# Attention's output turned by float32 products with stacked unit matrices, in place of transposes and additions

## The chip, the cores and the metric

One core of one Trainium2 chip runs the whole program. The metric is the device time of one execution in microseconds; lower is better. The kernel before was timed three times, and one more execution was profiled.

## The reference, cut to what matters

Four batches of eight heads of attention with rotary positions (sequence 576, head size 64) feed two gated layers over 2304 tokens. What the change touches is the last line of attention and the turn to tokens by features:

```python
scores = scale * np.matmul(q_rot, k_rot.transpose(0, 1, 3, 2))
scores = scores - np.max(scores, axis=-1, keepdims=True)
attn = np.exp(scores)
attn = attn / (np.sum(attn, axis=-1, keepdims=True) + 1e-09)
return np.matmul(attn, v).astype(np.float32)
...
x = np.ascontiguousarray(attn_out.transpose(0, 2, 1, 3)).reshape(B * S, H * D)
x = _moe_ref(x=x, **moe_kwargs)
return _moe2_ref(x=x, **moe2_kwargs)
```

## The kernel before, in words

**Precision.** TensorE multiplies float32r values, a shortened float32. To keep float32's precision, each operand is split into two float32r halves, hi (a rounding, on ACT) and lo (the rest, a subtraction on DVE), and a product is made of three products of halves (`PASS`: hi by hi, hi by lo, lo by hi). Transposes move whole float32 values (L598, L679, L709, L749, L771, L1226), except those at L1608, which are of float32r.

**Attention's stage.** The 32 heads are worked as 16 pairs `p`. A pair has nine tiles `t` of 128 rows of scores: four of each head, and tile 4, the left-over 64 rows of both. For each tile: S (scores, into one of two double banks of PSUM), M (negative row maximum, DVE), E (exponential and row sum, ACT), T (four transposes of P, into one of four PSUM banks `ps_g`), H and Lo (the split of P into `pt`, ACT and DVE). LP, LH and LL do the same for the 64 left-over columns. The Q and K of the next pair are turned (q0 to q2: qp on TensorE, qh on ACT, ql on DVE) and moved to their places by DMAs (q1d, q2d, L617).

**O.** For head `h` and half `hf` of the 576 queries, PV (L735) has as its stationary operand V's hi columns beside V's lo columns (64 + 64), and as its moving operand P. So its result has V's feature on the partitions: 64 rows of P by V's hi, and below them 64 rows of P by V's lo, which must be added to give O. OS (L740, ACT) copies it to `osb`, 128 x 576. O (L746 to L749) turns it: four transposes of 128x128 into one bank, after which each row is a query and has 64 hi features and 64 lo features. OA (L751, ACT) copies the lo features, 256 a partition, to `x`; OR (L754, DVE) adds the hi features to them and is the last to read the bank. OL (L768) turns the left-over 64 queries of both heads (two transposes), and OLR (L774, DVE) adds their halves in one reduction. RS (POOL) and RR (DVE) make 1/sum of each row, X (L790, POOL) multiplies, XD (L798) sends the pair's 128 features to `xD` in DRAM by two DMAs on SP's queue.

**Order.** The order is written by hand: `ORDER` (L18) gives each step a time in tiles, and step `n` of pair `p` is issued at `9 * p + ORDER[n]`, sorted by this time; each engine then works its own instructions in this order. In a pair's frame O0 stands at 14.022, OL at 15.595 and O1 at 16.188, so within the next pair at 5.0, 6.6 and 7.2; the S0 of the pair after that stands at 6.93 (9 - 2.067), right behind OL. The last pair's steps past the end of attention go to a planner (`Plan`), with the costs in `TAIL` (L74) and the dependences listed there; it keeps TensorE's order and arranges the other engines' work between the first products of the next layer. `tail_op` (L1061) also tells the planner which PSUM bank a step holds.

**After attention** TensorE multiplies for the two layers, in products of 384 or 256 columns (L1099, L1125, L1345, L1492, L1652, L1725); ACT, DVE and POOL split and combine.

Of the kernel before, what the change touches and what calls it, by code (L numbers as in the profile page):

```python
# [8 lines left out]
F32 = mybir.dt.float32  # L9
# [4 lines left out]
ALU = mybir.AluOpType  # L14
AX = mybir.AxisListType
# [15 lines left out]

ONCE = {"WF.0": 1.47, "WF.1": 1.48, "W0.0": 10.0, "W1.0": 12.2, "W2.0": 13.4, "W0.1": 11.6, "W3.0": 16.7,
# [41 lines left out]
TAIL = {"H": ("ACT", 0.6, ()), "Lo6": ("DVE", 0.65, ("H6",)), "Lo7": ("DVE", 0.65, ("H7",)), "Lo8": ("DVE", 0.65, ("H8",)),  # L74
# [5 lines left out]
PRI = 100  # L80
FIRST = {"q2p": -0.115, "q0p": -0.114, "q2h": -0.112, "q0h": -0.111, "q2l": -0.06, "q0l": -0.05, "q2d": -0.03,
    "q1p": 1.2, "q1h": 1.25, "q1l": 1.44, "q1d": 1.45}
# [5 lines left out]
def f(ap):  # L88
    return ap.bitcast(F32)
# [187 lines left out]
def kernel(  # L277
# [21 lines left out]
    nc = tc.nc  # L299
    B, H, S, D = q.shape  # L300
# [25 lines left out]
    const = ctx.enter_context(tc.tile_pool(name="const", bufs=1))  # L326
# [16 lines left out]
    idn = f(idr)  # L343
    g_sb = const.tile([128, DM], F32, name="g")
    cst = const.tile([128, 4], F32, name="cst")
    half, three, one, eps = [cst[:, i:i + 1] for i in range(4)]

    def opener(st):
# [28 lines left out]
    tab_p = pool("tab", 1)  # L377
    rightx = ctx.enter_context(ExitStack())
    rpool = lambda name, bufs: rightx.enter_context(tc.tile_pool(name=name, bufs=bufs, side="right", reuse_waits="tile"))
    ss_p = rpool("ss", 2)  # L380
    mem = []

    def grow():
# [130 lines left out]
    part = {}  # L514
# [122 lines left out]
    s_ps, s_max, p_sb, sums, t_ps, l_ps, pv_ps, osb, xt, o_ps, rs_t = [{} for _ in range(11)]  # L637
# [88 lines left out]
    def head_steps(h):  # L726
        def pv(hf):
            sl = slice(hf * HS, (hf + 1) * HS)

            def PV(p):  # L730
                vs = vss[p]
                ps = pv_ps[p, h, hf] = ps_g.tile([128, 512], F32, tag="g", name="pv")
                mm = [(vs[:, h, c], pt[:, 1 - h, i, c, sl]) for c in range(4) for i in range(2)] + [(vs[:, h, 4], lt[:, 1 - h, sl])]
                for i, (l, r) in enumerate(mm):
                    nc.tensor.matmul(ps[:, 0:HS], lhsT=l.rearrange("p s d -> p (s d)"), rhs=r, start=(i == 0), stop=(i == 8))  # L735

            def OS(p):
                if (p, h) not in osb:
                    osb[p, h] = osb_p.tile([128, S], F32, tag="o", name="osb")
                nc.scalar.copy(out=osb[p, h][:, sl], in_=pv_ps.pop((p, h, hf))[:, 0:HS])  # L740

            part[f"PV{h}{hf}"], part[f"OS{h}{hf}"] = PV, OS

        pv(0), pv(1)

        def O_(p):  # L746
            ps = o_ps[p, h] = ps_g.tile([128, 4, 128], F32, tag="g", name="op")
            for r in range(4):
                nc.tensor.transpose(ps[:, r], osb[p, h][:, r * 128:(r + 1) * 128], idn)  # L749

        def OA(p):  # L751
            nc.scalar.copy(out=xh_(p)[:, 0:4, h], in_=o_ps[p, h][:, :, D:128])

        def OR(p):  # L754
            nc.vector.tensor_tensor(out=xh_(p)[:, 0:4, h], in0=o_ps.pop((p, h))[:, :, 0:D], in1=xh_(p)[:, 0:4, h], op=ALU.add)

        part[f"O{h}"], part[f"OA{h}"], part[f"OR{h}"] = O_, OA, OR

    def xh_(p):
        if p not in xt:  # L760
            xt[p] = x_p.tile([128, 5, 2 * D], F32, tag="x", name="x")
        return xt[p].rearrange("p r (h d) -> p r h d", d=D)

    head_steps(0), head_steps(1)


    @step
    def OL(p):  # L768
        ps = o_ps[p, 2] = ps_g.tile([128, 4, 128], F32, tag="g", name="op")
        for h in range(2):  # L770
            nc.tensor.transpose(ps[:, h], osb[p, h][:, S - 128:S], idn)  # L771

    @step
    def OLR(p):  # L774
        nc.vector.tensor_reduce(out=xh_(p)[:, 4], in_=o_ps.pop((p, 2))[:, 0:2].rearrange("q r (s d) -> q r d s", s=2), axis=AX.X, op=ALU.add)  # L775

    @step
    def RS(p):
# [83 lines left out]
    ident = p_p.tile([128, S], F32, tag="p", name="ident")[:, 0:128]  # L862
    make_identity(nc, ident)
    nc.vector.tensor_copy(out=idr, in_=ident)
    man = ExitStack()
    man.enter_context(tc.manual_schedule())
    load(0)
# [86 lines left out]
    for p in range(NP):  # L954
        for n_, t in ORDER.items():
            d = 2 if n_ in ("ra", "rb", "rc", "rd", "lq", "lv") else 1 if n_[0] in "qv" else 0
# [37 lines left out]
    for u in range(6, 9):  # L994
        i, s = divmod(u, 3)
# [18 lines left out]
    def key(sp, i, n=1):  # L1014
        return sp, i, i + n
# [39 lines left out]
    def gslot():  # L1055
        gb[0] += 1
        return key("g", (gb[0] - 1) % 4)
# [3 lines left out]
    def tail_op(n_):  # L1061
        eng, dur, deps = TAIL["H" if n_[0] == "H" else n_]
        wr = []
        if n_ in ("PV11", "PV10", "O0", "OL", "O1"):
            tails["slot", n_] = gslot()
            wr = [tails["slot", n_]]
        for a, b in (("OS11", "PV11"), ("OS10", "PV10"), ("OA0", "O0"), ("OR0", "O0"), ("OLR", "OL"), ("OA1", "O1"), ("OR1", "O1")):
            if n_ == a:
                wr = [tails["slot", b]]
        if n_ == "XD":  # L1070
            wr = [key("xD", 13, 5)]
        tails[n_] = plan(eng, dur, lambda: part[n_](NP - 1), (), wr, dep=[tails[d] for d in deps if d in tails], kb=288 if n_ == "XD" else 0)
# [4 lines left out]
    def tail_to(n_):  # L1077
        while names and (n_ is None or n_ in names):
            tail_op(names.pop(0))
# [10 lines left out]
    def products_b(si, i, n, s):  # L1090
        sl = gslot()
        w, x = wgv[n], xg[i]

        def go():
            p_ = ps_ap[si, s] = ps_g.tile([128, 512], F32, tag="g", name="mm")[:, 0:CH]
            j = 0
            for c in range(KC):
                for a, b_ in PASS:
                    nc.tensor.matmul(p_, lhsT=w.ap[:, a, s, c * 128:(c + 1) * 128], rhs=x.ap[:, b_, c, :], start=(j == 0), stop=(j == 3 * KC - 1))  # L1099
                    j += 1  # L1100
        mark(plan("PE", 12 * MM, go, [w.part(s, 4), w.part(2 + s, 4), x.part()], [sl]))
        return sl
# [309 lines left out]
    for si, (i, n) in enumerate(steps):  # L1412
        if si == 0:
            units_to(9)
        g = products_b(si, i, n, 0)
# [404 lines left out]
```

## Time and profile before

| | us |
|---|---|
| median of three runs | 1051.91 |
| lowest, highest | 1051.77, 1054.71 |
| the profiled execution | 1052.25 |
| its span, first to last instruction | 1050.5 |
| attention's stage in it (pairs in full flow) | 27 to 312 |

The profile shows one execution. "Busy" is the time in which an engine works on at least one instruction; PE is TensorE's products, PEld its weight loads, which run beside them. A product's end is modelled, so neighbours overlap in the rows, and the distance between starts says more than the length. "<-" after a wait names what ended it. `op` is the PSUM tile of O and OL, `x` the result of OA, OR and OLR.

### The profile page before, as it was taken

The page shows a single profiled execution, that of the slowest core. Times are in us where ns is not written, and L with a number is a line of the kernel's source. Part 1 is how long each engine was busy: PE and PEld are TensorE (multiplying, and loading weights), DVE is VectorE, ACT ScalarE, POOL GpSimd, SP SyncE. Part 2 cuts the span into 40 slices and gives each one's busy share as a digit, 9 for nine tenths or more (in the row PEclk, how much of TensorE's full clock was granted, in tenths as well). Part 3 has the DMA queues.
Part 4 walks back from the last instruction along what each step waited for, and adds up shares of the span by engine and source line. Part 5 has one row for each costly group of instructions (what it writes and reads, how often), then busy time and mean ns, then how long its engine had stood idle before and what let it go on. Part 6 is the DMA issues. An engine that isn't in the chain of part 4 may idle for free.

```text
span 1050.5 us, 19662 instructions
## 1 busy us (share of the span) xinstructions
PE 1032.5 (98%) x6969; PEld 1022.7 (97%) x6969; DVE 810.4 (77%) x1394; ACT 656.6 (63%) x1442; POOL 378.1 (36%) x495
## 2 busy tenths in 40 slices
PE   7999999999999999999999999999999999999998
PEld 6999999999999999999999999999999999999997
DVE  7999999999987966779888778432576567998653
ACT  6898999898978654457666666332554344575430
POOL 7878888889610002543212230001522111410000
PEclk9999999999999999999999999999999999999999
DMA  6777877777669887279897967571342326445761
GB/s 159 210 203 195 221 174 183 185 190 181 176 212 308 280 261 235 81 237 314 292 355 246 317 206 226 185 238 46 106 158 106 154 73 214 176 148 211 270 219 61
DMA packets 125986, 210.41 MB, mean 200 GB/s; under 512 B 19136, under 2 KB 71744, under 8 KB 125888
## 3 DMA queue, kind: packets, MB, share of 16 engines
q1 hardware_dynamic: 125456, 208.71, 63.8%
q8 instruction: 55, 0.90, 0.4%
q10 hardware_dynamic: 432, 0.44, 0.1%
q14 instruction: 43, 0.35, 0.1%
HBM read 117.62 MB, written 63.96 MB: 173 GB/s over the span
## 4 chain that ended last, share of the span: by engine, by line
PE 87%; DVE 6%; DMA 3%; ACT 2%; issue 1%; SPq 1%; DVEq 0%; ACTq 0%
PE ps L1345 33%; PE mm L1099 10%; PE ps L1492 10%; PE ps L1725 9%; PE s L662 5%; PE acc L1125 5%; PE pv L735 4%; PE ps L1652 4%; PE tp L679 4%; DMA ks<-xy 2%; DVE nm L667 2%; DVE pt L687 2%; PE qtp L598 1%; PE lp L709 1%; PE op L749 1%
## 5 line engine op out<-in xcount | busy, mean ns | idle before, releaser
L1032 DVE TENSOR_TENSOR v<-v 128x256 fp32r<-128x256 f32 (+8 forms) x424 | 286.4, 704 | 94.7 <-ACT v L1026 92.2
L1345 PE MATMUL ps<-v 128*128 128x384 f32 x2016 | 350.7, 334 | 0.8 <-ACT ps L1026 0.8
L1345 PEld LDWEIGHTS ps<-v 128*128 128x128 f32 x2016 | 349.3, 188 | 1.5 <-ACT ps L1026 1.5
L1032 POOL TENSOR_TENSOR v<-v 128x256 f32<-128x256 f32 (+1 forms) x140 | 136.5, 992 | 475.5 <-DVE v L1032 185.0
L1026 ACT CAST v<-v 128x256 fp32r<-128x256 f32 (+5 forms) x364 | 203.3, 589 | 129.4 <-DMA v<-uG 41.0
L1032 DVE TENSOR_TENSOR v<-ps,v 128x384 f32<-128x384 f32 (+3 forms) x162 | 89.1, 572 | 75.7 <-PE ps L1345 36.8
L1026 ACT COPY v<-ps 128x384 f32<-128x384 f32 (+2 forms) x130 | 62.4, 482 | 112.6 <-PE ps L1345 58.5
L662 PE MATMUL s<-ks,qs 128*128 128x288 f32 x640 | 119.9, 313 | 6.4 <-ACT p L673 3.0
L667 DVE TENSOR_REDUCE nm<-s 128x1 f32<-128x576 f32 x144 | 107.8, 749 | 7.7 <-PE s L662 5.4
L673 ACT ACTIVATE p<-s,nm 128x576 f32<-128x576 f32 x144 | 107.4, 746 | 9.4 <-DVE nm L667 8.6
L1099 PE MATMUL mm<-v 128*128 128x384 f32 x576 | 104.2, 335 | 0.0
L1492 PE MATMUL ps<-v 128*128 128x384 f32 x576 | 100.0, 334 | 0.0
L1099 PEld LDWEIGHTS mm<-v 128*128 128x128 f32 x576 | 99.9, 188 | 0.0
L1492 PEld LDWEIGHTS ps<-v 128*128 128x128 f32 x576 | 99.9, 188 | 0.0
L662 PEld LDWEIGHTS s<-ks,qs 128*128 128x128 f32 x640 | 89.5, 189 | 10.1 <-ACT p L673 6.1
L687 DVE TENSOR_TENSOR pt<-tp,pt 128x512 fp32r<-128x512 f32 x144 | 94.6, 681 | 0.7
L1725 PE MATMUL ps<-v 128*128 128x256 f32 x756 | 90.9, 283 | 0.0
L1725 PEld LDWEIGHTS ps<-v 128*128 128x128 f32 x756 | 90.8, 192 | 0.0
L679 PE MATMUL tp<-idr,p 128*128 128x128 f32 x576 | 81.9, 273 | 1.1 <-DVE x L775 0.7
L683 ACT CAST pt<-tp 128x512 fp32r<-128x512 f32 x144 | 82.3, 585 | 1.0 <-PE tp L679 0.2
L735 PE MATMUL pv<-pt,vs 128*128 128x288 f32 x512 | 80.9, 300 | 0.1
L735 PEld LDWEIGHTS pv<-pt,vs 128*128 128x128 f32 x512 | 70.9, 188 | 0.3 <-DVE pt L687 0.3
(131 smaller groups left out, 1263.3 us busy)
## 6 DMA issues: line engine op xcount, KB each, us to landing
ks<-xy SPq DMA_DIRECT2D x60, 288.0 KB, 5.2
v<-in_moe_w_dram SPq DMA_DIRECT2D x32, 512.0 KB, 6.3
v<-in_moe_w_out_dram SPq DMA_DIRECT2D x20, 512.0 KB, 6.0
qs<-xy SPq DMA_DIRECT2D x60, 160.0 KB, 3.3
uG<-v SPq DMA_DIRECT2D x24, 384.0 KB, 4.7
v<-uG SPq DMA_DIRECT2D x24, 384.0 KB, 3.7
uD<-v SPq DMA_DIRECT2D x12, 768.0 KB, 3.5
v<-uD SPq DMA_DIRECT2D x12, 768.0 KB, 6.6
```

The costliest lines, as they stand in the source:

```text
L662: nc.tensor.matmul(ps[:, hf, 0:HS], lhsT=l, rhs=r_[:, hf * HS:(hf + 1) * HS], start=(i == 0), stop=(i == n - 1))
L667: nc.vector.tensor_reduce(out=nm, in_=s_ps[p, t][:, :, 0:HS], axis=AX.XY, op=ALU.max, negate=True)
L673: nc.scalar.activation(out=pp.rearrange("p (a b) -> p a b", a=2), in_=s_ps.pop((p, t))[:, :, 0:HS], func=AF.Exp, bias=s_max.pop((p, t)), s ...
L679: nc.tensor.transpose(ps[:, c, :], p_sb[p, t][:, LF + c * 128:LF + (c + 1) * 128], idn)
L687: lastins["dve"] = nc.vector.tensor_tensor(out=lo, in0=src, in1=f(hi), op=ALU.subtract)
L735: nc.tensor.matmul(ps[:, 0:HS], lhsT=l.rearrange("p s d -> p (s d)"), rhs=r, start=(i == 0), stop=(i == 8))
L1026: return plan("ACT", act_us(n), lambda: nc.scalar.copy(out=o(), in_=i()), rd, wr)
L1032: lambda: eng.tensor_tensor(out=o(), in0=x(), in1=y(), op=op), rd, wr)
L1099: nc.tensor.matmul(p_, lhsT=w.ap[:, a, s, c * 128:(c + 1) * 128], rhs=x.ap[:, b_, c, :], start=(j == 0), stop=(j == 3 * KC - 1))
L1345: nc.tensor.matmul(p_(), lhsT=w[i].ap[:, a, c * 128:(c + 1) * 128], rhs=x[i].ap[:, r, c], start=(first and ch != 1 and n == 0), stop=(n == 5),
L1492: nc.tensor.matmul(ac[o][ch][0](), lhsT=w.ap[:, a, o * 128:(o + 1) * 128], rhs=u.ap[:, b_, ch], start=(j == 0 and s == 0), stop=(j == NF - ...
L1725: nc.tensor.matmul(p_()[:, k * 256:(k + 1) * 256], lhsT=u.ap[:, a, UOP[i], o * 128:(o + 1) * 128], rhs=w(b_), start=(g == 0 and s == 0 and ...
```

## The change

A constant `both` (128 x 64, float32) holds two unit matrices above each other. O and OL are no longer transposes but products: stationary operand the same 128x128 piece of `osb`, moving operand `both`. Row q, column d of the result is `osb[d, q] + osb[64 + d, q]`: turned and added at once, 64 columns a piece in place of 128. OA copies the finished 256 values; OR is gone; OLR is a copy. `both` is made by one addition of two halves of the unit matrix at the start. The pool `ss` has one buffer in place of two. The planner's list loses OR0 and OR1, and its other costs are kept.

```diff
-    "PV10": 13.085, "OS10": 13.618, "O0": 14.022, "OA0": 15.251, "OL": 15.595, "OR0": 15.671, "O1": 16.188,
-    "RR": 16.466, "lv": 16.571, "OLR": 16.975, "OA1": 16.977, "OR1": 17.165, "X": 17.215, "XD": 17.967}
+    "PV10": 13.085, "OS10": 13.618, "O0": 14.022, "OA0": 15.251, "OL": 15.595, "O1": 16.188,
+    "RR": 16.466, "lv": 16.571, "OLR": 16.975, "OA1": 16.977, "X": 17.215, "XD": 17.967}
...
-    "OR0": ("DVE", 0.4, ("OA0",)), "OL": ("PE", 0.22, ("OS01", "OS11")), "OLR": ("DVE", 0.35, ("OL",)), "O1": ("PE", 0.44, ("OS10", "OS11")),
-    "OA1": ("ACT", 0.4, ("O1",)), "OR1": ("DVE", 0.4, ("OA1",)), "RS": ("POOL", 0.6, ()), "RR": ("DVE", 0.2, ("RS",)),
-    "X": ("POOL", 1.5, ("OR0", "OR1", "OLR", "RR")), "XD": ("SP", 0.8, ("X",))}
+    "OL": ("PE", 0.22, ("OS01", "OS11")), "OLR": ("DVE", 0.35, ("OL",)), "O1": ("PE", 0.44, ("OS10", "OS11")),
+    "OA1": ("ACT", 0.4, ("O1",)), "RS": ("POOL", 0.6, ()), "RR": ("DVE", 0.2, ("RS",)),
+    "X": ("POOL", 1.5, ("OA0", "OA1", "OLR", "RR")), "XD": ("SP", 0.8, ("X",))}
...
+    both = const.tile([128, D], F32, name="both")
...
-    ss_p = rpool("ss", 2)
+    ss_p = rpool("ss", 1)
...
         def O_(p):
-            ps = o_ps[p, h] = ps_g.tile([128, 4, 128], F32, tag="g", name="op")
+            ps = o_ps[p, h] = ps_g.tile([128, 512], F32, tag="g", name="op")[:, 0:4 * D].rearrange("q (r d) -> q r d", d=D)
             for r in range(4):
-                nc.tensor.transpose(ps[:, r], osb[p, h][:, r * 128:(r + 1) * 128], idn)
+                nc.tensor.matmul(ps[:, r], lhsT=osb[p, h][:, r * 128:(r + 1) * 128], rhs=both, start=True, stop=True)
 
         def OA(p):
-            nc.scalar.copy(out=xh_(p)[:, 0:4, h], in_=o_ps[p, h][:, :, D:128])
-
-        def OR(p):
-            nc.vector.tensor_tensor(out=xh_(p)[:, 0:4, h], in0=o_ps.pop((p, h))[:, :, 0:D], in1=xh_(p)[:, 0:4, h], op=ALU.add)
+            nc.scalar.copy(out=xh_(p)[:, 0:4, h], in_=o_ps.pop((p, h)))
...
     def OL(p):
-        ps = o_ps[p, 2] = ps_g.tile([128, 4, 128], F32, tag="g", name="op")
+        ps = o_ps[p, 2] = ps_g.tile([128, 512], F32, tag="g", name="op")[:, 0:2 * D].rearrange("q (h d) -> q h d", d=D)
         for h in range(2):
-            nc.tensor.transpose(ps[:, h], osb[p, h][:, S - 128:S], idn)
+            nc.tensor.matmul(ps[:, h], lhsT=osb[p, h][:, S - 128:S], rhs=both, start=True, stop=True)
...
     def OLR(p):
-        nc.vector.tensor_reduce(out=xh_(p)[:, 4], in_=o_ps.pop((p, 2))[:, 0:2].rearrange("q r (s d) -> q r d s", s=2), axis=AX.X, op=ALU.add)
+        nc.vector.tensor_copy(out=xh_(p)[:, 4], in_=o_ps.pop((p, 2)))
...
+    nc.vector.tensor_tensor(out=both, in0=ident[:, 0:D], in1=ident[:, D:2 * D], op=ALU.add)
```

## Rows read from the trace of the kernel before

**Rows 1.** The page's first part: engines over the whole span.
```profile
PE 1032.5 (98%) x6969; PEld 1022.7 (97%) x6969; DVE 810.4 (77%) x1394; ACT 656.6 (63%) x1442; POOL 378.1 (36%) x495
```

**Rows 2.** Stretches: us, busy us of each engine (instructions), granted clock, DMA share, GB/s.
```profile
core 0: us, PE busy (x) PEld busy (x) DVE busy (x) ACT busy (x) POOL busy (x), PEclk, DMA share, GB/s
27.00:312.00 285.00, 279.81 (x2221) 273.45 (x2222) 270.80 (x479) 259.12 (x636) 219.30 (x324) 1.00 0.74 194
...
312.00:345.00 33.00, 33.00 (x199) 32.90 (x198) 27.00 (x60) 23.39 (x54) 2.06 (x2) 1.00 0.88 298
345.00:400.00 55.00, 55.00 (x336) 54.90 (x334) 42.99 (x81) 33.06 (x62) 0.00 (x0) 1.00 0.87 278
400.00:700.00 300.00, 299.24 (x1725) 298.63 (x1725) 220.93 (x392) 170.54 (x370) 75.41 (x80) 1.00 0.74 243
```

**Rows 3.** TensorE's waits, 27 to 312 us: us in total, times, longest.
```profile
PE s L662 <- DMA ks<-xy: 2.3, 4, 1.3
PE op L749 <- DVE pt L687: 0.9, 2, 0.5
PE tp L679 <- DVE x L775: 0.7, 2, 0.4
PE s L662 <- DMA qs<-xy: 0.7, 1, 0.7
PE op L771 <- DVE lt L717: 0.2, 1, 0.2
PE s L662 <- ACT p L673: 0.2, 1, 0.2
PE s L662 <- issue: 0.2, 1, 0.2
```

**Rows 4.** Instructions on tile `op`: ns least/median/most, first and last start, forms.
```profile
L749 PEld LDWEIGHTS op<-idr,osb x128: 137/139/146, 42.1 to 309.5; 128*128 128x128 f32 x128
L749 PE MATMUL op<-idr,osb x128: 270/272/332, 42.2 to 309.6; 128*128 128x128 f32 x128
L771 PEld LDWEIGHTS op<-idr,osb x32: 137/140/143, 43.8 to 309.1; 128*128 128x128 f32 x32
```

**Rows 5.** The chain that ended last, 112 to 120 us: start, us, what.
```profile
114.46 0.44 PE op L749 x4
114.89 1.19 PE pv L735 x9
116.08 0.22 PE op L771 x2
116.30 0.16 issue
116.46 0.76 PE s L662 x4
```

**Rows 6.** The chain at 879 us, and the weight loads of line 1608.
```profile
879.50 1.31 PE ps L1608 x16
...
L1608 PEld LDWEIGHTS ps<-idr,v x64: 137/140/143, 879.2 to 931.2; 128*128 128x128 f32 x64
```

**Rows 7.** The chain of the whole span: products of 384 and of 256 columns.
```profile
461.93 172.13 PE ps L1345 x990
...
954.58 90.73 PE ps L1725 x756
```

**Rows 8.** Instructions on tile `x`: ns least/median/most, first and last start, forms.
```profile
L752 ACT COPY x<-op x32: 360/372/373, 44.3 to 309.9; 128x256 f32<-128x256 f32 x32
L755 DVE TENSOR_TENSOR x<-op,x x32: 406/414/425, 45.1 to 312.4; 128x256 f32<-128x256 f32 x32
...
L775 DVE TENSOR_REDUCE x<-op x16: 362/412/415, 46.7 to 311.4; 128x128 f32<-128x256 f32 x16
```

**Rows 9.** DVE's groups by shape, 27 to 312 us: busy us, mean ns, idle before.
```profile
L607 DVE TENSOR_TENSOR xy<-qtp,xy 128x128 fp32r<-128x128 f32 x14 | 4.1, 291 | 0.5 <-ACT xy L602 0.5
```

**Rows 10.** All engines' waits, 27 to 312 us: us in total, times, longest.
```profile
ACT x L752 <- PE op L749: 6.6, 14, 1.7
```

**Rows 11.** DVE's instructions in order of time, 0 to 16 us: start, us, what, idle before.
```profile
1.45 0.16 DVE L864 CAST idr<-ident 128x128 fp32r<-128x128 f32 x1
4.16 0.69 DVE L544 TENSOR_TENSOR rot<-raw,cos 128x512 f32<-128x512 f32 x1 [2.54 <-DMA raw<-in_k_dram]
```

More of the change, by code (lines that the diff above doesn't have):

```diff
@@ L746, in O_ @@
         def O_(p):
-            ps = o_ps[p, h] = ps_g.tile([128, 4, 128], F32, tag="g", name="op")
+            ps = o_ps[p, h] = ps_g.tile([128, 512], F32, tag="g", name="op")[:, 0:4 * D].rearrange("q (r d) -> q r d", d=D)
             for r in range(4):
-                nc.tensor.transpose(ps[:, r], osb[p, h][:, r * 128:(r + 1) * 128], idn)
+                nc.tensor.matmul(ps[:, r], lhsT=osb[p, h][:, r * 128:(r + 1) * 128], rhs=both, start=True, stop=True)
         def OA(p):
-            nc.scalar.copy(out=xh_(p)[:, 0:4, h], in_=o_ps[p, h][:, :, D:128])
-        def OR(p):
-            nc.vector.tensor_tensor(out=xh_(p)[:, 0:4, h], in0=o_ps.pop((p, h))[:, :, 0:D], in1=xh_(p)[:, 0:4, h], op=ALU.add)
-        part[f"O{h}"], part[f"OA{h}"], part[f"OR{h}"] = O_, OA, OR
+            nc.scalar.copy(out=xh_(p)[:, 0:4, h], in_=o_ps.pop((p, h)))
+        part[f"O{h}"], part[f"OA{h}"] = O_, OA
     def xh_(p):
@@ L1066, in tail_op @@
             wr = [tails["slot", n_]]
-        for a, b in (("OS11", "PV11"), ("OS10", "PV10"), ("OA0", "O0"), ("OR0", "O0"), ("OLR", "OL"), ("OA1", "O1"), ("OR1", "O1")):
+        for a, b in (("OS11", "PV11"), ("OS10", "PV10"), ("OA0", "O0"), ("OLR", "OL"), ("OA1", "O1")):
             if n_ == a:
```

## The prediction, made before the change was run

> **What bounds the kernel now.** I read the shares of the whole span first, then the stretches, then the stage that the change touches. Over the span TensorE is drawn busy 98% and DVE 77% [rows 1]; that is an average over stages. The stretches separate them [rows 2]. From 312 us on TensorE is busy without a gap worth naming (33.00 of 33, 55.00 of 55, 299.24 of 300), so whatever the attention stage gains or loses is passed on to the end one for one. In the attention stage (27 to 312 us) three engines run close together: TensorE 279.81 of 285, DVE 270.80, ACT 259.12. TensorE's granted clock is 1.00 in each of them, its 2.4 GHz level. So the question is which of TensorE and DVE paces this stage. TensorE is idle 5.2 us in it; by its weight loads (273.45) it is 11.5 us. The drawn end of a matmul lies after the point at which the next may start, so the truth lies between. TensorE's own list of waits [rows 3] says for what: 1.8 us behind DVE (0.9 + 0.7 + 0.2), 3.0 us behind the DMAs that move the split Q and K (2.3 + 0.7, five waits), the rest 0.4. I conclude that **TensorE paces attention**, with DVE just behind: an instruction added to TensorE costs its full length, less what of these few waits it covers; one taken off DVE returns at most these waits.
>
> **TensorE's part.** Removed: 128 transposes at L749 and 32 at L771 [rows 4]; added: 160 float32 products of the same stationary tile (128x128 of `osb`) with a moving tile of 64 columns in place of 128. What a transpose costs is read from the chain, where its modelled tail doesn't count: four take 0.44 us, two 0.22 [rows 5], so 0.110 each, 17.6 us in all. The trace has no float32 product that isn't a transpose: every other group's operands are float32r. So I bound it.
> - Low end: one weight load and one short product. The nearest row is the float32r transposes at L1608, sixteen in 1.31 us, 0.082 each [rows 6]. By columns alone a 64-column product would be shorter still: 990 products of 384 columns take 172.13 us (0.174 each) and 756 of 256 take 90.73 (0.120) [rows 7], 0.42 ns for a column. On that line 128 columns would be 0.067; L1608's 0.082 stands above it, so for short products something else than columns sets the pace, and I take it (an estimate) to be the weight load. With the same load, 64 columns don't go below 0.082.
> - High end: this kernel itself writes a product of two float32 values as products of their float32r halves (three, `PASS`). Should the engine do all four, each with its own weight load, a product costs 4 x 0.082 = 0.328.
> - My value is between: `osb` as weights in two halves, so two loads, and past each of them the 64 columns of `both` in two halves. That is 128 columns behind each load, what a product at L1608 has, so 2 x 0.082 = **0.164**. L749's weight loads are drawn as long as L1608's (139 and 140 ns) [rows 4, 6], which is why I use its rate.
>
> So each product costs 0.054 more than the transpose it replaces, and 160 cost **8.6 us more**. Four in O then take 0.66 in place of 0.44, two in OL 0.33 in place of 0.22: 0.54 us a pair of heads. Between the bounds: from 160 x (0.082 - 0.110) = -4.5 us to 160 x (0.328 - 0.110) = +34.9.
>
> The Trainium skill (FP8 and Floating Point Precision, TensorE Precision Notes) says that a true float32 product takes four passes through the array. If passes were all that counted, 4 x 64 columns at the 0.42 ns above would be an estimate of 0.107 us, the transpose's price. No row here shows such a product; as a result of its own it is the first rival below.
>
> **DVE's part.** Removed: 32 additions (OR) of 414 ns, 13.2 us [rows 8]. OLR's reduction of 412 ns becomes a copy of the same 128 results out of PSUM; the nearest row is the subtraction of 128x128 from PSUM, 291 ns [rows 9]. I take that as its upper bound, the lower being none, so at least 16 x 0.12 = 2.0 us go. DVE is relieved of 15.2 us, 0.95 for a pair, and its share of the stage falls from 95% to some 88%. On the path this is worth only the waits of TensorE that DVE ends: the 1.8 us [rows 3] go. They are waits for a PSUM bank that DVE frees; with OR gone an O bank is free when ACT has copied it.
>
> **Waits behind O and OL.** The next S stands right behind OL in TensorE's order, and it is there that the Q and K moves are waited for: in the chain OL is followed by 0.16 us of no work and then S [rows 5]. O0 and OL now take 6 x 0.054 = 0.32 us more ahead of that S, so each of the five waits gives back up to 0.32: 1.6 us. Together **3.4 us come back**. If DVE's earlier split of Q also brings the moves forward, the rest of the 3.0 goes too; that is the lower edge of my case.
>
> **ACT, POOL, SP and the start.** OA copies the same 256 elements of a partition (372 ns at most [rows 8]), from another part of the bank: nothing. It waits for O, which is longer: ACT waited for O 14 times, 6.6 us in all [rows 10], and 32 times 0.22 is 7.0 more at the worst. Behind OA in its queue stand exponentials, which S's banks wait for. ACT has 26 us free (285 - 259.12) [rows 2] and TensorE itself is later by the same amount, so nothing is added. X on POOL no longer waits for OR; POOL is at 219.30 of 285 and TensorE doesn't wait for it in this stage. X's DMAs go out a little earlier on SP, and move no more. `both` is one DVE instruction of 128x64 before the first load is there: DVE idles 2.54 us for K from 1.6 us on [rows 11], which hides 0.2; were that cover gone, it would cost 0.2 once. The planner's list loses OR0 and OR1 and keeps its other estimates; in the tail TensorE's order is given, and ten of the 160 products lie there at full price. Halving the pool `ss` binds nothing: its tiles are taken once each, or with one buffer already.
>
> **The sum.** 1052.25 (profiled execution) + 8.6 - 3.4 = 1057.45. That execution is 0.34 above the median of the three runs, 1051.91; against the median it is **1057.1**, 0.5% slower. About 0.3% (3.2 us, so 1048.8 to 1055.1) is what counts as no change here.
>
> **Rivals.**
> - *The product costs what the transpose cost, 0.110.* Four passes of half the columns. For it: the page's count; against it: L1608's 0.082 is above its own columns' share, so loads are likely to count. TensorE then has nothing added, and the waits behind DVE (1.8) and some of those behind the moves (up to 3.0) go: 1047.1 to 1050.1, middle 1048.6, faster. Chance 0.22.
> - *The product costs two full transposes, 0.220,* if each half is as slow as a float32 transpose, or more. For it: at 128 columns float32 takes 0.110 where float32r takes 0.082. +17.6, less 1.8 and five waits of up to 0.66 (2.6 in all): 1065.1. Chance 0.13. At the high end of 0.328 it would be some 1082.
> - *DVE is the pace after all.* DVE at 95% is held up by TensorE only little, and what TensorE waits for is DVE's lateness at one or two steps' remove. The relief of 15.2 us then clears all 11.5 us of idle time by the weight loads: 8.6 - 11.5 = -2.9, 1049.0, no change or just faster. It decides if the relief per pair, 0.95, reaches TensorE and exceeds the added 0.54. Against it: only 1.8 us of TensorE's waits name DVE. Chance 0.10.
> - *The change doesn't do what it says:* the product runs as one product of reduced precision, 0.082. Then -4.5 - 3.0 gives 1044.4. Chance 0.05; the operands' type in the diff speaks against it.
>
> **How the numbers follow.** My case, 1057.1, has 0.50; its own range is 1054 to 1062 (the rest of the DMA waits below, 0.19 per product above). About 0.06 of it lies within 0.3%. Faster: 0.14 of the first rival, 0.02 of the third, 0.05 of the fourth: 0.21. Same: 0.08 of the first, 0.08 of the third, 0.06 of mine: 0.22. Slower: 0.44 of mine and the second's 0.13: 0.57. The range reaches from the first rival's lower edge to just above the second: 1047 to 1066; it leaves out the fourth rival and prices over 0.22.
>
> **What would show it.** Right: in the changed profile TensorE has more weight loads for O than the 160 of before, four O products take about 0.66 us in the chain, DVE in attention falls by about 15 us, and the end of attention moves by about 5 us with everything behind it unchanged. Wrong: O's four products in 0.44 or less (first or fourth rival), in 0.88 or more (second), or TensorE's idle time falling by far more than 3.4 us (third). If S begins to wait for exponentials that stand behind OA, my zero for ACT is wrong.

## The result, and the profile after

The changed kernel takes 1062.28 us in the median of four runs (1061.99 to 1063.04), against 1053.31 (1051.77 to 1056.26) for the kernel before beside it: a ratio of 1.0086, 95% interval 1.0065 to 1.0106. It is slower by some 9 us (by the interval 6.8 to 11.2); 1057.1 was forecast, with a range of 1047 to 1066. The profiled execution of the changed kernel took 1062.24 us with a span of 1060.5, 10.0 us longer than before's.

Line numbers have moved: L750 is the product of O, L769 that of OL, L753 OA, L773 OLR. The page's first part, over the whole span:

```profile
PE 1046.8 (99%) x7129; PEld 1039.7 (98%) x7129; DVE 799.2 (75%) x1363; ACT 658.5 (62%) x1442; POOL 382.6 (36%) x495
```

TensorE has 160 products more than before [rows 1]: each of the 160 new ones is recorded as two, each with its own weight load. DVE has 31 recorded instructions fewer and is busy 11.2 us less: the instructions that went were drawn 15.3 us longer in all than what came for them, but neighbours on DVE are drawn over each other. The stretches, with the same columns as [rows 2]:

```profile
27.00:312.00 285.00, 284.46 (x2322) 281.28 (x2322) 251.06 (x425) 252.95 (x622) 219.37 (x323) 1.00 0.72 184
322.00:400.00 78.00, 78.00 (x474) 77.79 (x473) 60.13 (x122) 52.24 (x107) 0.00 (x0) 1.00 0.86 282
400.00:700.00 300.00, 298.78 (x1720) 297.60 (x1719) 225.13 (x401) 173.74 (x375) 77.91 (x80) 1.00 0.74 245
```

Over the same 285 us of attention TensorE's idle time has fallen from 5.2 to 0.5 us (by its weight loads from 11.5 to 3.7), while DVE's busy time fell by 19.7, partly since attention is stretched. Attention ends 9.0 us later: the first eight transposes behind it, before and after.

```profile
316.17 0.87 PE xp L1226 x8
325.17 0.87 PE xp L1225 x8
```

The last 1.0 us of the span came behind attention, some 0.8 of it between 455 and 510 us, where TensorE waits for ACT a little longer than before; whether that has to do with the change was not tried. From 510 us on it is as full as before. This stretch, before and after:

```profile
455.00:510.00 55.00, 54.24 (x312) 53.63 (x311) 49.51 (x90) 36.80 (x85) 17.94 (x18) 1.00 0.92 300
455.00:510.00 55.00, 53.78 (x308) 52.81 (x307) 45.92 (x79) 33.95 (x78) 22.60 (x22) 1.00 0.82 274
```

TensorE's own waits from 27 to 322 us are two lines, where seven stood before [rows 3]:

```profile
PE s L663 <- DMA qs<-xy: 0.7, 1, 0.7
PE op L750 <- DVE pt L688: 0.4, 1, 0.4
```

The instructions on the tiles `op` and `x` (ns least, median, most; first and last start; forms), for [rows 4, 8]:

```profile
L750 PEld LDWEIGHTS op<-both,osb x256: 186/192/192, 41.9 to 318.5; 128*128 128x128 f32 x128
L750 PE MATMUL op<-both,osb x256: 217/275/323, 42.0 to 318.6; 128*128 128x64 f32 x128
L769 PEld LDWEIGHTS op<-both,osb x64: 187/192/192, 44.0 to 317.6; 128*128 128x128 f32 x64
L753 ACT COPY x<-op x32: 362/373/376, 44.1 to 318.9; 128x256 f32<-128x256 f32 x32
L773 DVE COPY x<-op x16: 275/281/292, 46.5 to 318.7; 128x128 f32<-128x128 f32 x16
```

A weight load here is drawn 192 ns long; a transpose's was 139. OA costs what it did, OLR 281 ns in place of 412. In the kernel before, the loads of products were drawn as long already, PV's for one; those of LP's transposes, 64 columns wide, were drawn 111, and the chain has four of these transposes in 0.44 us as well:

```profile
L735 PEld LDWEIGHTS pv<-pt,vs x512: 186/188/193, 24.9 to 304.1; 128*128 128x128 f32 x171
L709 PEld LDWEIGHTS lp<-idr,p x144: 108/111/113, 20.0 to 294.0; 128*64 128x64 f32 x144
108.62 0.44 PE lp L709 x4
```

The chain at a pair in mid-attention, for [rows 5]:

```profile
115.06 0.84 PE op L750 x8
115.90 1.24 PE pv L736 x9
117.14 0.39 PE op L769 x4
117.53 0.58 PE s L663 x4
118.11 0.84 PE op L750 x8
```

Four products in O take 0.84 us where four transposes took 0.44, two in OL 0.39 for 0.22. The PV behind O takes 1.24 for 1.19, and the S behind OL 0.58 for 0.53 (0.53 is what an S takes elsewhere in this chain): the first one there comes late too. So a pair has 0.45 more at O0 with its PV, 0.22 at OL with its S and 0.40 at O1, 1.07 us; for 16 pairs **17.1 us were added on TensorE; 9.0 of them came out at the end of attention, and the span is 10.0 longer**. Two things remain to be shown: what sets the price of a product, and who gave the other 8.1 us back (7.1 by the span). These figures are from one profile of each kernel, and the times of the kernel before vary: its medians beside the changed kernel and the experiments run from 1050.58 to 1053.31. (The expectations below, written from the first reading of the chain, put them at 15.5 and 5.5, without the late loads.)

### The profile page after: what moved, and what is told of

It is laid out like the page before. It is cut to its first block, busy times and chain, and to the rows that moved or that the text cites. A ratio compares the mean times of both kernels' runs of the same rounds, so it can differ in the third digit from the quotient of the medians.

```text
span 1060.5 us, 19934 instructions
## 1 busy us (share of the span) xinstructions
PE 1046.8 (99%) x7129; PEld 1039.7 (98%) x7129; DVE 799.2 (75%) x1363; ACT 658.5 (62%) x1442; POOL 382.6 (36%) x495
## 4 chain that ended last, share of the span: by engine, by line
PE 95%; DMA 2%; DVE 2%; ACT 1%; issue 0%; SPq 0%; DVEq 0%; ACTq 0%
PE ps L1344 31%; PE mm L1098 9%; PE ps L1491 9%; PE ps L1724 9%; PE s L663 8%; PE pv L736 7%; PE tp L680 6%; PE acc L1124 4%; PE ps L1651 4%; PE op L750 3%; PE lp L710 1%; PE qtp L599 1%; DMA v<-in_moe_w_dram 1%; PE xp L1225 1%; PE op L769 1%; PE ps L1607 0%
## 5 line engine op out<-in xcount | busy, mean ns | idle before, releaser
L1031 POOL TENSOR_TENSOR v<-v 128x256 f32<-128x256 f32 (+1 forms) x140 | 140.4, 1020 | 474.3 <-DVE v L1031 193.7
L668 DVE TENSOR_REDUCE nm<-s 128x1 f32<-128x576 f32 x144 | 108.2, 752 | 28.1 <-PE s L663 13.8
```

What stands on the lines that cost most here:

```text
L668: nc.vector.tensor_reduce(out=nm, in_=s_ps[p, t][:, :, 0:HS], axis=AX.XY, op=ALU.max, negate=True)
L1031: lambda: eng.tensor_tensor(out=o(), in0=x(), in1=y(), op=op), rd, wr)
```

## Experiments

Two theories for these 7 to 8 us. A: TensorE paces attention, and its few waits were covered since TensorE itself came later. B: DVE's relief removed them. For the price: weight loads, or columns.

**DVE's relief alone.** The transposes stay; OA takes the hi half, OR is gone, OLR is a copy.

```diff
-            nc.scalar.copy(out=xh_(p)[:, 0:4, h], in_=o_ps[p, h][:, :, D:128])
-        def OR(p):
...
+            nc.scalar.copy(out=xh_(p)[:, 0:4, h], in_=o_ps.pop((p, h))[:, :, 0:D])
...
+        nc.vector.tensor_copy(out=xh_(p)[:, 4], in_=o_ps.pop((p, 2))[:, 0:2, 0:D])
```

> The kernel before with DVE's part of the change alone: O is still transposed, the additions OR are gone, OLR is a copy; the lo half of V's part is left out of O. TensorE's work is unchanged. Theory A (TensorE paces attention, and the waits went in the changed kernel because TensorE itself came later): only the waits that DVE ends go, 1.8 us, and a part of the 3.0 for the moved Q and K: 2 to 4 us faster than before, near 1050. Theory B (the 5.5 us that came back in the changed kernel, 15.5 added on TensorE against 10.0 in the span, are DVE's relief): 5.5 us faster or more, 1048 or less.

Measured: 1050.40 in the median of twelve runs against 1051.99, ratio 0.9989 (0.9973 to 1.0004). By the ratio that is 1.2 us, at most 2.8, and possibly nothing. The stretch and TensorE's waits in it:

```profile
27.00:312.00 285.00, 278.40 (x2222) 272.81 (x2222) 259.52 (x449) 258.93 (x639) 219.98 (x324) 1.00 0.74 194
...
PE s L662 <- ACT osb L740: 2.0, 2, 1.1
PE s L662 <- DMA ks<-xy: 1.8, 2, 1.6
PE op L749 <- DVE pt L687: 1.4, 1, 1.4
PE s L662 <- ACT p L673: 0.8, 2, 0.7
```

DVE has 11 us less to do in the stretch than before, and TensorE is idle 6.6 us, not less than before's 5.2. (The profiled execution took 1053.25, near the upper end of its twelve runs. Its attention began late: its first transpose of O starts at 45.2 us, before's at 42.2. From there to the product that follows the last O, L1122 here and L1125 before, it takes 266.7 us, before's 267.4.) The waits named after DVE's OLR are gone; others, after ACT and the moved K, stand in their place. Theory B asked for 5.5 us or more and falls; A's 2 to 4 was a little too much too.

**TensorE's part alone.** The float32 products, with DVE's 48 instructions kept in their shapes.

```diff
+                nc.tensor.matmul(ps[:, r, 0:D], lhsT=osb[p, h][:, r * 128:(r + 1) * 128], rhs=both, start=True, stop=True)
...
+            nc.scalar.copy(out=xh_(p)[:, 0:4, h], in_=o_ps[p, h][:, :, 0:D])
         def OR(p):
             nc.vector.tensor_tensor(out=xh_(p)[:, 0:4, h], in0=o_ps.pop((p, h))[:, :, 0:D], in1=xh_(p)[:, 0:4, h], op=ALU.add)
...
```

> TensorE's part of the change alone: the float32 products as in the changed kernel, but DVE's 32 additions and its 16 reductions stay, with the same shapes (they add O to itself, so O is doubled). Theory A: the waits are covered all the same, so the time is that of the changed kernel within 1.5 us, 1061 to 1064. Theory B: nothing relieves DVE, so up to 5.5 us more than the changed kernel, 1066 to 1068.

Measured: 1062.97 in the median of five runs, ratio 1.0106 (1.0087 to 1.0124), beside the changed kernel's 1062.28 and 1.0086 (1.0065 to 1.0106). A's number; the 0.7 us between the two medians lies within their noise, and fits the relief alone. With DVE's additions in place TensorE is as full as in the changed kernel:

```profile
27.00:312.00 285.00, 284.14 (x2312) 280.66 (x2313) 265.44 (x453) 252.93 (x619) 219.14 (x323) 1.00 0.71 181
```

**The same load without any float32 product.** The kernel before, each transpose of O and OL issued twice.

```diff
+                for _ in range(2):
                     nc.tensor.transpose(ps[:, r], osb[p, h][:, r * 128:(r + 1) * 128], idn)
...
```

> The kernel before with each of O's and OL's transposes issued twice to the same place: 17.6 us more on TensorE in the places where the change added 15.5, no float32 product and no relief of DVE. Theory A: some 5 us of waits are covered, 12 to 13 us slower than before, 1064 to 1066. Theory B: DVE's load keeps the waits, 16 to 17.6 slower, 1068 to 1070.

Measured: 1061.42 in the median of four against 1050.58, ratio 1.0100 (1.0083 to 1.0117): 10.8 us slower, its profiled span 9.8 us longer than before's.

```profile
27.00:312.00 285.00, 284.28 (x2315) 281.22 (x2316) 264.81 (x455) 253.46 (x621) 219.94 (x323) 1.00 0.71 183
```

160 transposes at 0.110 are 17.6 us; some 7 to 8 of them were covered, and with DVE's full load. (A had said some 5 and 12 to 13 us slower, so its number was missed too, on the side away from B.) So the cover needs neither the float32 product nor DVE's relief: it is TensorE's own idle time, which any work in these places fills. By the weight loads it goes from 11.5 to 3.8 us in this stretch, 7.7 us, and that is about what came back.

**A product twice.** The changed kernel with each product issued twice.

```diff
+                for _ in range(2):
                     nc.tensor.matmul(ps[:, r], lhsT=osb[p, h][:, r * 128:(r + 1) * 128], rhs=both, start=True, stop=True)
...
```

> The changed kernel with each of the 160 products issued twice to the same place. If TensorE now paces all of attention and one product costs 0.21 us on the path, 160 x 0.21 = 33.6 us more, 1095 to 1097. If products hide behind DVE or ACT anywhere, less: each us short of 33.6 is a us that was hidden. If ACT's waits for O add to it, more.

Measured: 1097.84 in the median of four, ratio 1.0433 (1.0414 to 1.0451); the profiled span, 1096.1, is 35.6 us longer than the changed kernel's. For 160 products that is 0.222 each, with nothing hidden. The chain at one pair:

```profile
104.68 1.88 PE op L751 x16
106.56 1.24 PE pv L736 x9
107.80 0.84 PE op L771 x8
108.64 0.58 PE s L663 x4
109.22 1.73 PE op L751 x16
```

The second eight halves of O1 add 0.89 us to the first eight's 0.84, so in steady flow a half (one of the two recorded products) takes 0.111. (O0's 1.88 holds a wait in this pair; in the next two it is 1.73 as well.) Once TensorE has no idle time left, every further microsecond on it is one on the kernel. The changed kernel's next cost would be paid in full.

**One load in place of two.** `osb` and `both` in float32r.

```diff
-    both = const.tile([128, D], F32, name="both")
+    both = const.tile([128, D], F32R, name="both")
...
-                osb[p, h] = osb_p.tile([128, S], F32, tag="o", name="osb")
+                osb[p, h] = osb_p.tile([128, S], F32R, tag="o", name="osb")
```

> The changed kernel with osb and the stacked unit matrices in float32r: each product becomes one load and one product of 64 columns (O is rounded to float32r). If the weight load sets a short product's price, it is 0.082 as at the float32r transposes or 0.105 as a half of the float32 product: 13 to 17 us in place of the transposes' 17.6, so with DVE's relief 1044 to 1050. If columns set it, 64 x 0.42 ns and some 0.013 over, 0.04: 6.4 us, TensorE is 11 us lighter than before and DVE or ACT paces; 1042 to 1045, and the chain shows four products in 0.16.

Measured: 1049.00 in the median of ten against 1051.99, ratio 0.9975 (0.9964 to 0.9987). The chain:

```profile
113.83 0.36 PE op L750 x4
114.20 1.26 PE pv L736 x9
115.46 0.14 PE op L769 x2
115.60 0.64 PE s L663 x4
```

Four products of one load seem to take 0.36, and two 0.14, but the work behind them is longer by what they are shorter: O0 with its PV is 1.62 here and 1.63 before (0.44 + 1.19, [rows 5]), OL with its S 0.78 and, with an undelayed S of 0.53, 0.75; O1 with its LP is 0.83 (0.37 + 0.46) for 0.88. From O0 to the S behind LP a pair takes 3.13 us here at the least, and 3.17 before. So a product of one load and 64 columns costs what a float32 transpose of 128 columns costs, to some 0.004 us, though it has half the columns. But the type changed as well, and a product took the transpose's place, so this run alone doesn't say what the columns count for. The time is that of DVE's relief alone (0.9989), the intervals overlapping. This kernel is faster than the kernel before and the changed one, but it rounds O to float32r, which those two don't.

**The price by itself.** Five bursts of twelve products at the start of the changed kernel.

```diff
+    for n_, w_, r_ in ((64, idn, idn), (32, idn, idn), (128, idn, idn), (64, idr, idr), (128, idr, idr)):
+        for _ in range(12):
+            nc.tensor.matmul(wps[:, 0:n_], lhsT=w_, rhs=r_[:, 0:n_], start=True, stop=True)
```

> The changed kernel with five bursts of twelve products at the very start, while the first loads are awaited: float32 by 64, 32 and 128 columns, float32r by 64 and 128. Their results are thrown away. It measures a price, not the time. If the weight load sets the price of a float32 half, halves stand 0.105 to 0.112 apart at 32 columns and at 64, and hardly more at 128; float32r products stand 0.08 apart at both sizes. If columns set it, a half at 32 columns takes half of that at 64, and 128 columns twice.

Groups of TensorE by shape (busy us, mean ns, idle before), first from 1 to 11.9 us, then 12.2 to 15.05 (float32, 128 columns), then 15.2 to 18.85 (the last of float32, then float32r by 64 and by 128), and the weight loads before and after 15.2 us:

```profile
L884 PE MATMUL warm<-idr 128*128 128x64 f32 x24 | 5.4, 423 | 1.7 <-DVE idr L862 1.7
L884 PE MATMUL warm<-idr 128*128 128x32 f32 x24 | 5.3, 400 | 0.0
...
L884 PE MATMUL warm<-idr 128*128 128x128 f32 x14 | 3.3, 431 | 0.0
...
L884 PE MATMUL warm<-idr 128*128 128x128 f32 x23 | 3.1, 286 | 0.0
L884 PE MATMUL warm<-idr 128*128 128x64 f32 x12 | 1.5, 277 | 0.0
...
L884 PEld LDWEIGHTS warm<-idr 128*128 128x128 f32 x63 | 13.5, 332 | 1.7 <-DVE idr L862 1.7
...
L884 PEld LDWEIGHTS warm<-idr 128*128 128x128 f32 x33 | 3.8, 194 | 0.0
```

Twelve float32 products are 24 recorded ones. Without the last one's drawn length, halves stand 0.22 us apart at 64 columns ((5.4 - 0.42) / 23), 0.21 at 32 ((5.3 - 0.40) / 23) and 0.22 at 128 ((3.3 - 0.43) / 13). From 15.2 us on the pace is about twice as fast: float32r products of 64 columns stand 0.111 apart ((1.5 - 0.28) / 11), what float32 halves take in steady flow, and by their starts in the trace the last float32 halves of 128 columns and the float32r products of 128 stand 0.11 apart too. So within one pace neither the columns, from 32 to 128, nor the type changes the price: **a recorded product with its weight load costs the same, whatever passes behind the load**. That it is the load itself, and nothing else that comes once with each such pair, is likely and not shown: no product here had a smaller load or none. The expected 0.105 to 0.112 for a half holds for the second pace, the expected 0.08 for float32r doesn't. The two paces are taken up at the end.

**OL alone.** The kernel before with the change in OL and OLR only.

```diff
-            nc.tensor.transpose(ps[:, h], osb[p, h][:, S - 128:S], idn)
+            nc.tensor.matmul(ps[:, h, 0:D], lhsT=osb[p, h][:, S - 128:S], rhs=both, start=True, stop=True)
...
```

> The kernel before with the change in OL and OLR alone: 32 products in place of 32 transposes, 2.7 us more on TensorE, all of them right ahead of the S behind which TensorE waited most; O and OR stay. If waits at that S are what covers the added work (the changed kernel's 5.5 us), the first 2.7 us are covered whole: no difference to before, within 1.5 us, and TensorE's idle time in the stage is smaller than before's 5.2 us by about 2. If the cover comes from elsewhere (around O's own places, or from DVE's relief), 2 to 3 us slower.

Measured: 1052.93 in the median of twelve against 1051.13, ratio 1.0012 (0.9999 to 1.0025): 1.3 us by the ratio, from nothing to 2.6 (the medians lie 1.8 apart). The stretch, and the one wait of TensorE for a move that is left in it:

```profile
27.00:312.00 285.00, 282.06 (x2260) 277.45 (x2259) 270.16 (x483) 260.15 (x638) 220.44 (x324) 1.00 0.75 195
...
PE s L663 <- DMA qs<-xy: 0.4, 1, 0.4
```

TensorE's idle time fell by 2.3 us, as expected, and S no longer waits for the moved K at all (2.3 us before, [rows 3]). The time lies at the edge of what was expected: the interval holds both a whole and half a cover. It says that part of the cover is at this S, and doesn't settle how much of it.

## Why the prediction was right, and where it was off

- **TensorE paces attention: held.** Double the products and every microsecond comes out (35.6 for 160 products at 0.222); take 11 us off DVE and 1.2 come back, the interval reaching to none. That attention's gain or loss is passed on one for one held but for the 1.0 us that the profiled execution lost behind attention.
- **What happens to a product: held.** Two weight loads, each with a product behind it, were the working of my value between the bounds; the record shows just that, x256 for 128 and x64 for 32. That 128 columns pass behind each load, as the working had it, is not shown: each recorded product is drawn with 64.
- **The price of a product was the term that was mis-sized:** 0.164 forecast, 0.21 in the chain and 0.222 in steady flow. The step that failed is "I use its rate", L1608's 0.082 for a weight load, on the ground that its loads are drawn as long as those of L749 [rows 4, 6]. The prediction's own rows spoke against that ground: at the same drawn length L749's transposes take 0.110 and L1608's 0.082 [rows 5, 6], so the drawn length of a load doesn't give its price. Besides, both are loads of transposes. The loads of products were drawn 188 ns before the change as well (L662, L735, L1099), and the new ones are at 192; I had taken the load of the operation that goes for the load of the one that comes. And LP's transposes, whose loads have 64 columns and are drawn 111 ns, take 0.11 all the same, so for float32 transposes it isn't the width of the load that sets the price. What the products' longer drawn load has to do with their 0.111 stays open. Behind products of 256 columns and more the price of a load can't be seen, since 0.120 and more [rows 7] pass there anyway. So 160 products cost 17.1 us more, where 8.6 were forecast.
- **The second rival had the better price,** 0.220: each half does take what a float32 transpose takes. Its ground, float32 being slower than float32r, holds for transposes and not for products (the bursts), and its return was too small: 1065.1.
- **The first rival fell.** Four passes over 64 columns, the Trainium skill's count (FP8 and Floating Point Precision, TensorE Precision Notes), would be the transpose's price, if passes alone counted. The bursts show that columns don't count up to 128: each recorded product with its load does. By the Trainium skill (TensorE: Matmul & The Clock Gate, LDWEIGHTS) a load of 128 columns takes 128 / 1.2, an estimate of 107 ns. The measured 0.111 of a product with its load is near it; the float32r transposes, 0.082 apart [rows 6] with loads of 128 columns, are below it.
- **The return was mis-sized too, the other way:** 3.4 us forecast, 8.1 measured at the end of attention (7.1 by the span). I counted the waits listed for products, 5.2 us in all [rows 3], and gave back 0.32 at each of five and 1.8 for DVE. The drawn end of a product hides the first part of each wait; the idle time by weight loads (11.5 us, to 3.7) was the better measure of what added work can fill. And I put those 1.8 us down to DVE's relief, which by its own run is worth 1.2, perhaps nothing: with the relief alone TensorE's idle time did not fall, and without it (TensorE's part alone, the transposes twice) it fell all the same.
- **The third rival, DVE as the pace, fell** with the relief alone, 0.9989 where it asked for the idle time to go. The sign that I had named for it did show, TensorE's idle time falling by more than 3.4 us (4.7, by weight loads 7.8); but it fell as much with DVE's full load (the transposes twice, 7.7), so the sign didn't tell the two apart.
- **ACT at nothing: held.** ACT's waits for O rose from 6.6 us in 14 to 16.0 in 17, and TensorE waited for an exponential once, 0.2 us by its weight loads. TensorE waited for POOL nowhere in the stage. POOL, the start and the last pair were not tried by themselves.

The two errors, 8.5 us too little added and 4.7 too little returned, partly cancel: 5.2 us forecast, 9.0 at the end of attention and in the medians, 10.0 in the profiled spans. So the direction, the engine that paces and the two loads were right, and the number owes something to luck: 1062.28 lies just above the 1054 to 1062 that my own case had, and is in the forecast's range since that reached up to the second rival. O's four products at 0.84 are also nearer to that rival's sign, 0.88, than to mine, 0.66.

## What to carry to other kernels

For a short product, count weight loads, not columns: with 32 to 128 moving columns each load of 128x128 with its product cost 0.11 us here, and a float32 product is two of them. Take the price of a new operation from rows of its own kind, and where a long neighbour hides it, say that it is hidden rather than take it from another kind. The length at which a load is drawn is not its price. Taking work off an engine at 95% brings little if another one paces; and the first microseconds added to an engine that paces with small gaps can be covered (some 8 of 17 here), the following ones are paid in full.

## What the runs showed that I had not expected

- **Float32r transposes stand closer together than float32r products.** L1608's stand 0.082 apart [rows 6], the products of 64 columns 0.111, with the same 128x128 stationary tile.
- **Where TensorE is full, the times vary less.** The kernel before ranged from 1048.98 to 1056.26 over its runs (51 of them), DVE's relief alone from 1047.73 to 1053.91 (12), OL alone from 1049.88 to 1054.89 (12); the changed kernel from 1061.99 to 1063.04, the transposes twice from 1061.13 to 1062.07, the products twice from 1097.38 to 1097.95 (4 each), TensorE's part alone from 1062.15 to 1064.29 (5). But the full ones have few runs, and one load in place of two, not full, stayed within 1048.23 to 1051.19 in ten. Why is not shown.
- **The bursts' pace doubles where the clock's record begins.** The same shape (float32, 128 columns) goes from 0.22 apart to some 0.12 at about 15.2 us ((3.1 - 2 x 0.28) / 21, for the row of 23, which has two bursts in it), and a load from 333 ns to 192, with TensorE at work without a gap since 1.67 us. The trace's record of the granted clock has its first entry at 15.2 us: 1.00, the 2.4 GHz level. Before that entry it has none, and the views print 1.00 there all the same. So the level before isn't recorded; a pace of about half fits the lower one, 1.2 GHz, and that is argued, not shown. The kernel before shows the same: its first transposes stand 0.213 apart, from 7 us on 0.109, and its record of the clock begins at 5.6 us.
- **Where the clock's record begins later, attention starts later.** It begins at 5.6 us in the profiles of before and after, at 10.2 with one load in place of two, at 10.9 with OL alone, at 13.8 with DVE's relief alone; their first transposes or products of O start at 42.2, 42.0, 43.1, 43.5 and 45.2 us. So up to 3 us between two profiled spans come from the start alone, and stages are better compared from their own first products on. What makes the record begin late, and whether it is what delays attention, was not tried.
